# The last weight matrix in two loads instead of three, and the wait for it moved from VectorE to TensorE

## The chip, the core and the metric

The kernel runs on one core of a Trainium2 chip. The metric is the device time in microseconds of one execution; the median of 3 runs of the kernel before is 189.54 us (189.49 to 189.69). Five engines take part: TensorE (PE, with weight loads shown as PEld), VectorE (DVE), ScalarE (ACT), GpSimd (POOL) and SyncE (SP), which issues nearly all DMA transfers. The core's transfers run on 16 DMA engines.

## The reference

One token passes through an attention block with a cache of keys and values and then through a small mixer and MLP block. Cut to what matters:

```python
x = A_x                                    # 1 x 1 x 512
h = x + attention(layernorm(x))            # 32 heads, 8 key heads, 16384 cached positions of 128
g0, g1, g2, g3 = shifted pieces of gelu(layernorm(h) @ w1)   # shifted along a sequence of length 1
x1 = h + concat(g0, g1, g2, g3) @ w2
h2 = gelu(layernorm(x1) @ w3) @ w4         # w3: 512 x 1792, w4: 1792 x 512
out = h + (x1 + h2)
```

With a sequence of one token every shift leaves zeros, so that the product with w2 is zero and x1 = h; the kernel loads neither w1 nor w2. What is left of the second block is the layer norm of h, the product with w3, the gelu, the product with w4 and the sums.

## The kernel before

The kernel streams 64 MB of keys and values, four pairs of key heads one after the other, and keeps the attention's weights and the last two matrices in the buffers that the keys used. For each pair, VectorE transposes the keys (L656), TensorE makes scores (L667), a softmax follows, and TensorE multiplies with the values (L708). The loop over the pairs on TensorE is a rolled loop with a register for the count that it waits for; the rest is straight code.

The order of the work is the order of the program: a small class records every operation with what it reads and writes, and puts before each instruction the waits for the semaphores of what it needs (on the same engine only where that is not in order anyway). Each load has a semaphore of its own, and one load counts as landed when all of its parts have landed. All loads of the tail go through the queue of SP, in the order in which they are written: `wo` in two loads, `w3` in one, `w4` in three. They are issued once the last keys have been read from the buffer that they overwrite, long before they are used.

The tail, behind the last values: VectorE gathers the attention's output, TensorE multiplies it with `wo` (L794), h is summed (L806), the norm's sums and square roots are made on VectorE (L540 to L582) while TensorE multiplies with `w3` (L819). Some matmuls whose result nobody reads (L518, `unread`) lie between. ScalarE then makes the gelu in two halves of 7 row blocks (L829), VectorE transposes each half into `hcol` (L833), and TensorE multiplies with `w4` (L845). `w4` has 1792 rows, held as 14 row blocks of 128 rows by 512 columns (`NHC` is 14), 128 KB each. For each block m there are four matmuls of 128 columns, one for each quarter of the output, which go to four different column groups of the array. They add onto h, which already stands in the same bank (`h_ps`). Before the last block, four weight loads stand by themselves (L841) and the block's matmuls go without theirs (`held`, L524), so that the weights are in before the wait for the block's data. Behind it, VectorE and ScalarE each copy half of the result (L852, L853) and SP stores it (L855).

What the loads' pieces are is set by these tables; `piece(W4, m)` gives the number of the load that holds block m, and key `("r", 1, len(W3) + n)` is that of load n of w4:

```python
W3 = ((0, 4),)
W4 = ((0, 8), (8, 13), (13, 14))
```

In the kernel before, the transpose of the gelu's first half also reads the key of w4's first load (the term `* (n == 0)` in L833), and the matmuls wait themselves only for the loads with a number above 0.

Of the kernel before, what the change touches and what calls it, by code (L numbers as in the profile page):

```python
# [358 lines left out]
NHC = FM // 128  # L359
# [4 lines left out]

SEEN, ROUND = 53, 28
W3 = ((0, 4),)
W4 = ((0, 8), (8, 13), (13, 14))
PAIRS = HKV // 2
WHOLE = (0, 2)
CUTS = ((0, 2, 4), (0, 4))  # L370
# [15 lines left out]
def bass_sequential_preLN__gqa_block_cached__mixer_s_mlp__decode_kernel(  # L386
# [13 lines left out]
    with ExitStack() as ctx:  # L400
# [52 lines left out]
        hg = sb("hg", [128, FQ], BF16)  # L453
        hT = sb("hT", [128, NCH, 32], FP32)
        hcol = sb("hcol", [128, NHC, 32], BF16)
# [7 lines left out]
        w4_sb = kb[1][:, NCH * FM:2 * NCH * FM].rearrange("p (m c) -> p m c", m=NHC)  # L463
# [9 lines left out]
        def load(name, dst, src, key, by="SP", also=()):  # L473
            P.op(by, lambda e: e.dma_start(dst, src), w=[key, *also], dma=name)  # L474
# [28 lines left out]
        def dve(fn, r=(), w=(), bank=(), own=None):  # L503
            return P.op("DVE", fn, r, w, bank, own=own)

        def act(fn, r=(), w=(), bank=(), own=None):
            return P.op("ACT", fn, r, w, bank, own=own)
# [4 lines left out]
        def pe(fn, r=(), w=(), bank=(), also=(), times=None, many=1):  # L512

            return P.op("PE", fn, r, w, bank, also=also, times=times, many=many)
# [6 lines left out]
        def held(e, out, lhsT, rhs, stop):  # L521
            with nc.discard():
                m = e.matmul(out, lhsT, rhs, start=False, stop=stop, skip_group_check=True).ins
            return e.add_instruction(mybir.InstMatmult(  # L524
                name=nc.get_next_instruction_name(), engine=m.engine, ins=m.ins, outs=m.outs, start_tensor_calc=False,
                stop_tensor_calc=m.stop_tensor_calc, tile_size=m.tile_size, tile_position=m.tile_position,
                bass_skip_group_check=True, ldweights=False))

        def piece(cuts, m):
            return [lo <= m < hi for lo, hi in cuts].index(True)  # L530
# [62 lines left out]
        for n in range(2):  # L593
# [8 lines left out]
            r=["ident_f", "x4"], w=["quarter"])  # L602
        pe(lambda e: e.matmul(O_ps[0][:, 0:128], quarter[:, :, :].rearrange("p q u -> p (q u)"), x4[:, :],  # L603
                              start=True, stop=True), r=["quarter"], w=[("O", 0)], bank=[("O", 0)])
# [7 lines left out]
            r=["ident_f"], w=["row32"])  # L612
        dve(lambda e: e.tensor_reduce(maskdd[:, :], ident_f[:, :].rearrange("p (n d) -> p d n", d=4), AX.X, ALU.add),
            r=["ident_f"], w=["maskdd"])
# [3 lines left out]
        for z, src, key, of, n in ((zo, row32[:, :].rearrange("p (g n h) -> p g h n", g=2, h=REP), "zo", "row32", 4),  # L618
# [6 lines left out]
            r=["hT", (("st", 0), 0), (("st", 0), 6), "wq0"] + [("v", x) for x in range(VP)], w=["xn"])  # L625
# [3 lines left out]
        for i, key in enumerate(keys):  # L629
            P.part("query", i)  # L630
            for k in range(NCH):
                pe(lambda e, k=k: e.matmul(row[:, bass.ds(P.b + P.b0, 512)], copies(xn[:, k:k + 1], 128),  # L632
                                           wq_k[:, k, bass.ds(P.c + P.c0, REP * DH)], start=(k == 0), stop=(k == NCH - 1)),
                   r=["xn"], also=[("v", x) for x in range(VP)], w=["n" if key == "mn" else key], bank=[key])
        P.part()
        for g in range(2):
            half = banks[64 * g:64 * g + 64, PAIRS * g:PAIRS * g + PAIRS, :].rearrange("p j c -> p (j c)")
            for b in range(2):
# [3 lines left out]
                    r=["n" if x == "mn" else x for x in keys[PAIRS * g:PAIRS * g + PAIRS]], w=["qcol"],  # L642
                    bank=keys[PAIRS * g:PAIRS * g + PAIRS])
        for a in range(4):
            lo, hi, at = 32 * a, 32 * a + 32, QPAD + 32 * a
# [137 lines left out]
        w4_in = B_w4.rearrange("(p m) c -> p m c", p=128)  # L783
        for n, (lo, hi) in enumerate(W4):
            load(f"w4{n}", w4_sb[:, lo:hi, :], w4_in[:, lo:hi, :], ("r", 1, len(W3) + n))
# [3 lines left out]
            r=["o_m"], w=["o_f"])  # L789
        dve(lambda e: e.tensor_copy(o_b[:, :], o_f[:, :]), r=["o_f", ("r", 0, 0)], w=["o_b"])  # L790

        for r_ in range(32):
# [3 lines left out]
                                              stop=(r_ < 4 or r_ >= 28), skip_group_check=(r_ >= 4)),  # L796
               r=["o_b"] + [("r", 0, n) for n in (piece(WO, r_),) if n], w=[("O", 0)], bank=[("O", 0)],
# [3 lines left out]
        h_ps, hkey = banks[:, 6, :], "spare0"  # L801
        for n in range(2):
            dve(lambda e, n=n: e.tensor_copy(osum[:, 256 * n:256 * n + 256], O_ps[0][:, 256 * n:256 * n + 256]),  # L803
                r=[("O", 0)], w=[("osum", n)], bank=[("O", 0)])
        for q in range(4):
            pe(lambda e, q=q: e.matmul(h_ps[32 * q:32 * q + 32, 0:128], copies(row32[:, 0:1], 32),  # L806
                                       osum[:, q * 128:(q + 1) * 128], start=True, stop=True),
               r=[("osum", q // 2), "row32"], w=[hkey], bank=[hkey])
# [4 lines left out]
            r=["hT", (S, 0)] + [("r", 1, 0)], w=["hc"])  # L813
# [3 lines left out]
        for k in range(NCH):  # L817
            for q in range(4):
                pe(lambda e, k=k, q=q: e.matmul(s_ps[32 * q:32 * q + 32, 0, 0:FQ], hc[:, k, :],  # L819
                                                w3_sb[:, k, q * FQ:(q + 1) * FQ], start=(k == 0), stop=(k == NCH - 1)),  # L820
                   r=["hc"] + [("r", 1, n) for n in (piece(W3, k),) if n], w=[("s", 0)], bank=[("s", 0)])
# [4 lines left out]
            r=["xs", (S, 6), "hr"], w=[hkey], bank=[hkey])  # L826
        for n in range(2):
            lo, hi = n * NHC // 2, (n + 1) * NHC // 2
            act(lambda e, lo=lo, hi=hi: e.activation(  # L829
                hg[:, :].rearrange("p (i m) -> p i m", m=NHC)[:, :, lo:hi],  # L830
                s_ps[:, 0, 0:FQ].rearrange("p (i m) -> p i m", m=NHC)[:, :, lo:hi],
                ACTF.Gelu_apprx_tanh, scale=s[:, 7:8]), r=[("s", 0), (S, 7)], w=[("hg", n)], bank=[("s", 0)])
            dve(lambda e, lo=lo, hi=hi: e.transpose(  # L833
                hcol[:, lo:hi, :].rearrange("p m u -> p (m u)"),
                hg[:, :].rearrange("p (i m) -> p m i", m=NHC)[:, lo:hi, :]), r=[("hg", n)] + [("r", 1, len(W3))] * (n == 0), w=[("hcol", n)])
        for m in range(NHC):
            if m == 4:
                pe(None)
            if m == NHC - 1:
                for o in range(4):  # L840
                    pe(lambda e, o=o: e.ldweights(hcol[:, NHC - 1, :], tile_position=(0, 32 * o)), r=[("hcol", 1)])  # L841
            for o in range(4):
                pe(lambda e, m=m, o=o: held(
                    e, h_ps[32 * o:32 * o + 32, 0:128], hcol[:, m, :], w4_sb[:, m, o * 128:(o + 1) * 128], True)
                    if m == NHC - 1 else e.matmul(  # L845
                    h_ps[32 * o:32 * o + 32, 0:128], hcol[:, m, :], w4_sb[:, m, o * 128:(o + 1) * 128],
                    start=False, stop=False, skip_group_check=True),
                   r=[("hcol", 2 * m // NHC)] + [("r", 1, len(W3) + n) for n in (piece(W4, m),) if n],
                   w=[hkey], bank=[hkey])


# [5 lines left out]
             r=[("fin", 0), ("fin", 1)], w=["out"], dma="out")  # L857
# [32 lines left out]
```

## Time and profile before

| what | value |
|---|---|
| median of 3 runs | 189.54 us (189.49 to 189.69) |
| profiled execution, span from first to last instruction | 188.3 us |
| median less that span | 1.24 us |
| read from HBM | 79.17 MB, 420 GB/s over the span |
| busy: PE, DVE, ACT, POOL | 66%, 62%, 7%, 2% |
| mean granted TensorE clock | 0.916 of full speed |
| tail: w4's matmuls, first start to last end | 185.34 to 186.78 us |

All times of the profile are counted from the start of its span. A row of the timeline holds the start, the time from the first start to the last end of the merged instructions, the engine, the line, the operation, output and inputs with their shapes, and the count; in brackets stands the idle time of the engine before it and what ended it. In a row of stretches the columns are the stretch, its length, then busy time and count for PE, PEld, DVE, ACT and POOL, the granted clock, the share of the DMA engines and their GB/s. In the chain of waits, a DMA's piece runs from its issue to its landing. A row of DMA issues gives the size and the time from issue to landing.

### The profile page before, as it was taken

Reading aid. Unit: us, or ns where it says so; the run is one execution under the profiler, and the core shown is the slowest. Engines: PE = TensorE matmul, PEld = TensorE weight load, DVE = VectorE, ACT = ScalarE, POOL = GpSimd, SP = SyncE. Lnnn points to the kernel's source line nnn. Section 1 sums busy time; section 2 is a strip of 40 time slices with the busy share of each in tenths; the row PEclk is TensorE's granted clock in tenths of the full one; section 3 lists DMA queues with packets and bytes.
Section 4 is the critical chain, followed back from the end, with each engine's and each line's share of the span. In section 5 each row is a group of like instructions: output and inputs, shape, how many; then the busy total and the mean of one; then the engine's idle time right before and its main releaser. Section 6 shows DMA issues by size and latency. Waiting matters only on the chain.

```text
span 188.3 us, 2375 instructions
## 1 busy us (share of the span) xinstructions
PE 124.1 (66%) x760; PEld 48.3 (26%) x761; DVE 115.8 (62%) x138; ACT 13.7 (7%) x21; POOL 4.6 (2%) x8
## 2 busy tenths in 40 slices
PE   0109700698979978897910019799799889775772
PEld 0104200233322522332500003333244333222221
DVE  5730741999636998936300069993699898633173
ACT  3000200000004000004000000000400000500012
POOL 8100000000000000000000000000000000000000
PEclk9999985569999999999995557999999999999999
DMA  7999999999799999987999999998999996999994
GB/s 252 445 418 445 445 445 446 445 445 445 334 445 446 445 557 418 418 390 334 446 445 445 445 446 445 445 445 334 445 446 445 543 390 292 445 432 411 433 429 193
DMA packets 2607, 79.19 MB, mean 421 GB/s; under 512 B 302, under 2 KB 430, under 8 KB 686
## 3 DMA queue, kind: packets, MB, share of 16 engines
q1 hardware_dynamic: 2598, 79.17, 98.0%
q8 instruction: 1, 0.02, 0.0%
q10 hardware_dynamic: 8, 0.00, 0.0%
HBM read 79.17 MB, written 0.00 MB: 420 GB/s over the span
## 4 chain that ended last, share of the span: by engine, by line
DMA 69%; DVE 23%; PE 4%; issue 3%; SPq 1%; DVEq 0%
DMA kb<-in_A_k_cache_dram 54%; DVE kt L656 22%; DMA kb<-in_B_w_dram 15%; PE banks L667 3%; SPq L474 1%; PE banks L845 0%; DVE fin L852 0%; DVEq L147 0%; DVE den L725 0%; PE banks L524 0%; DVE od L723 0%; SPq L147 0%
## 5 line engine op out<-in xcount | busy, mean ns | idle before, releaser
L667 PE MATMUL banks<-kt,qn 128*128 x256 | 68.1, 401 | 36.8 <-DVE kt L656 35.7
L656 DVE STREAM_TRANSPOSE kt<-kb 128x2048 int32<-128x2048 int32 (+2 forms) x24 | 70.6, 2994 | 27.5 <-DMA kb<-in_A_k_cache_dram 26.4
L667 PEld LDWEIGHTS banks<-kt,qn 128*128 x256 | 25.4, 100 | 79.4 <-issue 65.5
L518 PE MATMUL banks<-qb 128*128 128x512 bf16 x61 | 22.1, 387 | 0.7 <-issue 0.2
L708 PE MATMUL banks<-vb,pt 128*32 128x512 bf16 x256 | 14.7, 379 | 1.1 <-POOLq L500 1.1
L693 ACT ACTIVATE p_sb<-banks,bias 128x1024 bf16<-128x1024 f32 x4 | 4.5, 1114 | 133.3 <-DVE nmh L688 133.3
L632 PE MATMUL banks<-vb,xn 128*128 x32 | 8.5, 432 | 6.7 <-DVE xn L623 6.7
L697 DVE STREAM_TRANSPOSE pt<-p_sb 64x1024 bf16<-64x1024 bf16 x8 | 9.9, 1239 | 4.4 <-ACT p_sb L693 4.3
L681 DVE TENSOR_REDUCE mx<-banks 128x1 f32<-128x1024 f32 x4 | 4.9, 1224 | 10.5 <-PE banks L667 10.5
L518 PEld LDWEIGHTS banks<-qb 128*128 128x128 bf16 x62 | 5.9, 97 | 16.0 <-issue 15.7
L708 PEld LDWEIGHTS banks<-vb,pt 128*32 128x32 bf16 x256 | 8.5, 97 | 5.4 <-POOLq L500 1.2
L639 DVE STREAM_TRANSPOSE qcol<-banks 64x1024 f32<-64x1024 f32 x4 | 4.8, 1227 | 6.7 <-PE banks L632 6.7
L632 PEld LDWEIGHTS banks<-vb,xn 128*128 128x128 bf16 x32 | 3.5, 108 | 11.4 <-issue 8.7
L676 ACT ACTIVATE banks<-mean 128x1024 f32<-128x1024 f32 x4 | 4.1, 1027 | 18.6 <-DVE qcol L639 18.5
L684 PE MATMUL banks<-mxd,mean 128*128 128x128 f32 x8 | 2.0, 326 | 4.7 <-DVE mxd L682 4.7
L732 DVE SCALAR_TENSOR_TENSOR od<-banks,rowc,od 128x128 f32<-128x128 f32 x12 | 4.2, 350 | 0.4
L794 PE MATMUL banks<-kb,o_b 128*32 128x512 bf16 x44 | 3.3, 384 | 1.6 <-DVE o_b L790 1.1
L729 DVE TENSOR_SCALAR od<-banks,rowc 128x128 f32<-128x128 f32 x4 | 1.3, 319 | 4.6 <-PE banks L708 4.6
L603 PE MATMUL banks<-x,quarter 4*128 4x128 bf16 x1 | 0.3, 286 | 5.4 <-DVE quarter L601 5.4
L601 DVE CAST quarter<-ident_f 4x128 bf16<-4x128 f32 x1 | 2.9, 2901 | 1.3 <-DMA x<-in_A_x_dram 1.3
L737 PE MATMUL banks<-od,zo 128*32 128x128 f32 x10 | 2.0, 283 | 1.8 <-DVE od L732 1.6
L803 DVE COPY osum<-banks 128x256 f32<-128x256 f32 x2 | 0.8, 418 | 4.0 <-PE banks L794 4.0
(74 smaller groups left out, 39.5 us busy)
## 6 DMA issues: line engine op xcount, KB each, us to landing
kb<-in_A_k_cache_dram SPq DMA_DIRECT2D x4, 4096.0 KB, 20.5
vb<-in_A_wq_dram SPq DMA_DIRECT2D x1, 3584.0 KB, 11.7
kb<-in_A_wo_dram SPq DMA_DIRECT2D x1, 2560.0 KB, 26.2
kb<-in_B_w_dram SPq DMA_DIRECT2D x1, 1792.0 KB, 24.4
kb<-in_A_wo_dram SPq DMA_DIRECT2D x1, 1536.0 KB, 29.5
kb<-in_B_w_dram SPq DMA_DIRECT2D x1, 1024.0 KB, 26.6
kb<-in_B_w_dram SPq DMA_DIRECT2D x1, 640.0 KB, 27.7
vb<-in_A_wq_dram SPq DMA_DIRECT2D x1, 512.0 KB, 3.6
```

Source lines behind the costliest of these rows:

```text
L518: P.op("PE", lambda e: e.matmul(O_ps[1][:, :], field[:, 0:128], field[:, 0:512], start=True, stop=True), r=["qb"], bank=[("O", 1)], times= ...
L632: pe(lambda e, k=k: e.matmul(row[:, bass.ds(P.b + P.b0, 512)], copies(xn[:, k:k + 1], 128), wq_k[:, k, bass.ds(P.c + P.c0, REP * DH)], sta ...
L639: dve(lambda e, g=g, b=b, half=half: e.transpose(qcol[64 * g:64 * g + 64, 2 * b:2 * b + 2, :, :].rearrange("p e m u -> p (e m u)"), half.r ...
L656: P.op("DVE", lambda e, t=t, n=n: e.transpose(pieces(kt, t, n).bitcast(I32), pieces(kb[y], t, n).bitcast(I32)), r=[("r", y, i) for i in ra ...
L667: pe(lambda e, n=n: e.matmul(row[:, bass.ds(P.y, 512)], qn[:, n, bass.ds(P.q, 128)], key_piece(P.k, n), start=False, stop=(n == 3), skip_g ...
L676: act(lambda e: e.activation(s_all, copies(mean4[:, 0:1], 1024), ACTF.Identity, scale=0.0), r=["mean4", "p"], w=[("s", 0), ("s", 1)], **both)
L681: dve(lambda e: e.tensor_reduce(mx[:, :], s_all, AX.X, ALU.max), r=[("s", 0), ("s", 1)], w=["mx"], **both)
L693: act(lambda e: e.activation(p_sb[:, :], s_all, ACTF.Exp, bias=bias[:, 0:1], scale=float(SCALE), accum_out=acc[:, :]), r=[("s", 0), ("s", ...
L697: dve(lambda e, g=g: e.transpose(pt[64 * g:64 * g + 64, :, :, g, :], p_sb[64 * g:64 * g + 64, :]), r=["p"], w=["pt"])
L708: pe(lambda e, l=l, ct=ct, ch=ch: e.matmul(O_ps[0][32 * ct:32 * ct + 32, :], pt[:, l, ch, :, :].rearrange("p g u -> p (g u)"), tiles[:, l ...
L732: dve(lambda e, block=block, c=c: e.scalar_tensor_tensor(od[:, :], block, rowc[:, c:c + 1], od[:, :], ALU.mult, ALU.add), r=[key, "rowc", ...
L794: pe(lambda e, r_=r_, q=q: e.matmul(O_ps[0][32 * q:32 * q + 32, :], copies(o_b[:, r_:r_ + 1], 32), wo_sb[:, r_ * D:(r_ + 1) * D], start=(r ...
```

## The change

w4 comes in two loads, of blocks 0 to 11 and of blocks 12 and 13. The transposes of the gelu no longer read the key of w4's first load; every matmul of the last product reads the key of the load that holds its block. The weight loads that stand by themselves, and the matmuls without theirs, move from block 13 to block 12, the first of the last load; block 13 behind it is made of common matmuls, and the accumulation's end mark moves to it.

```diff
-W4 = ((0, 8), (8, 13), (13, 14))
+W4 = ((0, 12), (12, 14))
...
             dve(lambda e, lo=lo, hi=hi: e.transpose(
                 hcol[:, lo:hi, :].rearrange("p m u -> p (m u)"),
-                hg[:, :].rearrange("p (i m) -> p m i", m=NHC)[:, lo:hi, :]), r=[("hg", n)] + [("r", 1, len(W3))] * (n == 0), w=[("hcol", n)])
+                hg[:, :].rearrange("p (i m) -> p m i", m=NHC)[:, lo:hi, :]), r=[("hg", n)], w=[("hcol", n)])
         for m in range(NHC):
             if m == 4:
                 pe(None)
-            if m == NHC - 1:
+            if m == W4[-1][0]:
                 for o in range(4):
-                    pe(lambda e, o=o: e.ldweights(hcol[:, NHC - 1, :], tile_position=(0, 32 * o)), r=[("hcol", 1)])
+                    pe(lambda e, m=m, o=o: e.ldweights(hcol[:, m, :], tile_position=(0, 32 * o)), r=[("hcol", 1)])
             for o in range(4):
                 pe(lambda e, m=m, o=o: held(
-                    e, h_ps[32 * o:32 * o + 32, 0:128], hcol[:, m, :], w4_sb[:, m, o * 128:(o + 1) * 128], True)
-                    if m == NHC - 1 else e.matmul(
+                    e, h_ps[32 * o:32 * o + 32, 0:128], hcol[:, m, :], w4_sb[:, m, o * 128:(o + 1) * 128], False)
+                    if m == W4[-1][0] else e.matmul(
                     h_ps[32 * o:32 * o + 32, 0:128], hcol[:, m, :], w4_sb[:, m, o * 128:(o + 1) * 128],
-                    start=False, stop=False, skip_group_check=True),
-                   r=[("hcol", 2 * m // NHC)] + [("r", 1, len(W3) + n) for n in (piece(W4, m),) if n],
+                    start=False, stop=(m == NHC - 1), skip_group_check=True),
+                   r=[("hcol", 2 * m // NHC), ("r", 1, len(W3) + piece(W4, m))],
```

On SP, the last rows of the queue, from wo's second load on (`d_w40`, `d_w41`, `d_w42` below are the semaphores of w4's loads, `d_k1` that of the keys in the same buffer; a load of 128x4096 is 4096 elements of 2 bytes in each of 128 rows):

```order
 L474 DMA kb<-in_A_wo_dram 128x6144
 L474 DMA kb<-in_B_w_dram 128x7168 [waits e_DVE,d_k1]
-L474 DMA kb<-in_B_w_dram 128x4096
-L474 DMA kb<-in_B_w_dram 128x2560
-L474 DMA kb<-in_B_w_dram 128x512
+L474 DMA kb<-in_B_w_dram 128x6144
+L474 DMA kb<-in_B_w_dram 128x1024
 L855 DMA out_dram<-fin 2x2x128 [waits e_both]
```

Three loads of 1024, 640 and 128 KB became two of 1536 and 256 KB at the same place behind w3, and the first of them is as large, and has rows as long, as wo's second.

On TensorE, where the product with w4 begins (`e_DVE` is the semaphore that VectorE's instructions count up, `e_ACT` that of ScalarE's):

```order
 L819 MATMUL banks<-kb,hc 32x448 x15
-L845 MATMUL banks<-kb,hcol 32x128 [waits e_DVE]
+L845 MATMUL banks<-kb,hcol 32x128 [waits d_w40,e_DVE]
 L845 MATMUL banks<-kb,hcol 32x128 x15
 L344 COMPARE_AND_BRANCH
```

The wait for the first load now stands before the first of the 56 matmuls, beside the wait for the transposes.

On TensorE, from block 4 to the end of the product:

```order
 L845 MATMUL banks<-kb,hcol 32x128 x12
 L845 MATMUL banks<-kb,hcol 32x128 [waits e_DVE]
-L845 MATMUL banks<-kb,hcol 32x128 x3
-L845 MATMUL banks<-kb,hcol 32x128 [waits d_w41]
 L845 MATMUL banks<-kb,hcol 32x128 x19
 L841 LDWEIGHTS hcol x4
-L524 MATMUL banks<-kb,hcol 32x128 [waits d_w42]
+L524 MATMUL banks<-kb,hcol 32x128 [waits d_w41]
 L524 MATMUL banks<-kb,hcol 32x128 x3
+L845 MATMUL banks<-kb,hcol 32x128 x4
```

The wait before block 8 is gone, and the wait for the last load stands before block 12 with one more block behind it.

## The prediction

> **What bounds the kernel now.** I read the chain of waits first, then its last piece, then the timeline of that piece. The page's summary of the chain says how the whole run is bound:
>
> ```profile
> DMA 69%; DVE 23%; PE 4%; issue 3%; SPq 1%; DVEq 0%
> ```
>
> Nearly all of it is the stream of keys, values and weights from HBM, which the change leaves alone. The change touches what stands at the end of the chain. The chain in order of time, from 157.68 us on:
>
> ```profile
> 157.68 0.33 SPq L474
> 158.01 0.05 issue
> 158.06 0.43 SPq L474
> 158.48 0.05 issue
> 158.53 27.68 DMA kb<-in_B_w_dram
> 186.22 0.04 issue
> 186.26 0.46 PE banks L845 x20
> 186.73 0.07 PE banks L524 x4
> ```
>
> The load issued at 158.53 is the second of the three of w4 (blocks 8 to 12). It lands 27.68 us later, at 186.22, TensorE starts 0.04 us after, and the output follows. So the end hangs on landings and on the matmuls that are left behind the last landings. The page's list of DMA issues gives the landings of all four last loads:
>
> ```profile
> kb<-in_B_w_dram SPq DMA_DIRECT2D x1, 1792.0 KB, 24.4
> kb<-in_B_w_dram SPq DMA_DIRECT2D x1, 1024.0 KB, 26.6
> kb<-in_B_w_dram SPq DMA_DIRECT2D x1, 640.0 KB, 27.7
> kb<-in_B_w_dram SPq DMA_DIRECT2D x1, 128.0 KB, 27.5
> ```
>
> With the issue times of the chain: w3 (1792 KB) lands at 157.68 + 24.4 = 182.1, blocks 0 to 7 at 158.06 + 26.6 = 184.66, blocks 8 to 12 at 186.22. The last is issued behind those: 158.53 + 0.43 + 0.05 = 159.0, if its predecessor's issue takes as long as the one before it; + 27.5 gives 186.5. The timeline of the tail shows who waited for each:
>
> ```profile
> 183.65 0.85 ACT L829 ACTIVATE hg<-banks,st 128x224 bf16<-128x224 f32 x2 [0.75 <-PE banks L819]
> 184.71 1.05 DVE L833 STREAM_TRANSPOSE hcol<-hg 128x224 bf16<-128x224 bf16 x2 [1.04 <-DMA kb<-in_B_w_dram]
> 185.34 0.71 PE L845 MATMUL banks<-kb,hcol 128*32 128x128 bf16 x32 [1.75 <-DVE hcol L833]
> 186.26 0.46 PE L845 MATMUL banks<-kb,hcol 128*32 128x128 bf16 x20 [0.20 <-DMA kb<-in_B_w_dram]
> 186.56 0.22 PE L524 MATMUL banks<-kb,hcol 128*32 128x128 bf16 x4
> 186.82 0.27 ACT L853 ACTIVATE fin<-banks 64x128 bf16<-64x128 f32 x1 [2.32 <-PE banks L524]
> ```
>
> VectorE's transposes wait for the first load (to 184.71), TensorE's first 32 matmuls for the transposes (to 185.34); they are through at 185.34 + 0.71 = 186.05, and TensorE then idles 0.20 us for the second load. That idle gap is the first thing to see: **the transposes' wait is real, but it is not on the path that sets the end**. Its slack is 0.20 us. The other thing is at 186.56: 0.04 us after the last landing, the last four matmuls start; without that wait they would have started one step (0.055 us, below) behind the fifth block, at about the same time. Both landings end together for the end.
>
> **The change part by part.**
>
> *Transposes without the load's wait.* The gelu's two ACT instructions run 183.65 to 184.50. The first of two transposes then starts some 0.1 us after the first ACT half, near 184.2, instead of 184.71, and both are done about 1.05 us later, at 185.3. TensorE's start came 0.63 us behind the first transpose's (184.71 to 185.34), so hcol's first half is ready for it at 184.8 and the second by 185.3. The gain on the end is nothing, since TensorE's new first wait, for the load, ends later than both (next). Were that cover gone, the transposes would cost those 0.63 us. Nothing else is queued behind them on VectorE but the final CAST.
>
> *When 12 blocks have landed.* This is the term that decides, and I bound it in two ways. From the two landings here: 640 KB separate 184.66 from 186.22, that is 1.56 us for five blocks or 0.312 us a block. Four blocks behind the first landing is 184.66 + 1.25 = 185.91; one block ahead of the second is 186.22 − 0.31, the same 185.91. From a load of the same size and row length that this kernel already makes, the second of wo (the timeline's rows, then the page's):
>
> ```profile
> 147.92 0.80 SPq L474 DMA_DIRECT2D kb<-in_A_wo_dram  x2
> 157.68 1.77 SPq L474 DMA_DIRECT2D kb<-in_B_w_dram  x4
> 177.88 0.83 PE L794 MATMUL banks<-kb,o_b 128*32 128x512 bf16 x12 [0.53 <-DMA kb<-in_A_wo_dram]
> ```
>
> ```profile
> kb<-in_A_wo_dram SPq DMA_DIRECT2D x1, 2560.0 KB, 26.2
> kb<-in_A_wo_dram SPq DMA_DIRECT2D x1, 1536.0 KB, 29.5
> ```
>
> wo's first load lands at 147.92 + 26.2 = 174.1 and the reader of its second starts at 177.88, so that landed at 177.84: 3.7 us for 1536 KB behind its predecessor. Behind w3's 182.1 the twelve blocks then land at 185.8. Between 185.8 and 185.91 I take the middle, 185.85: the higher one comes from loads with shorter rows than the new load's, the lower one from landings that are rounded to 0.1 us. The lag of a landing behind its bytes is in both. It can be seen at the end:
>
> ```profile
> 184.60:184.80 0.20, 0.00 (x0) 0.00 (x0) 0.09 (x1) 0.00 (x0) 0.00 (x0) 1.00 0.98 410
> 185.80:186.00 0.20, 0.20 (x14) 0.10 (x4) 0.00 (x0) 0.00 (x0) 0.00 (x0) 1.00 0.64 220
> 186.00:186.20 0.20, 0.06 (x4) 0.00 (x0) 0.00 (x0) 0.00 (x0) 0.00 (x0) 1.00 0.04 10
> 186.20:186.40 0.20, 0.14 (x12) 0.14 (x16) 0.00 (x0) 0.00 (x0) 0.00 (x0) 1.00 0.00 0
> ```
>
> The last columns are the DMA share and GB/s: bytes stop near 186.05, while the last landing is seen at 186.5, 0.45 us later. [...]
>
> *What TensorE does from there.* All 14 blocks, 56 matmuls, now stand behind that landing, where 24 stood behind the second load before. Each block is four matmuls side by side; the timeline cut at three places gives its step:
>
> ```profile
> 186.26 0.24 PE L845 MATMUL banks<-kb,hcol 128*32 128x128 bf16 x4 [0.20 <-DMA kb<-in_B_w_dram]
> 186.26 0.46 PE L845 MATMUL banks<-kb,hcol 128*32 128x128 bf16 x20 [0.20 <-DMA kb<-in_B_w_dram]
> 185.34 0.57 PE L845 MATMUL banks<-kb,hcol 128*32 128x128 bf16 x28 [1.75 <-DVE hcol L833]
> ```
>
> One block takes 0.24, five 0.46, seven 0.57: 0.055 us a further block. Fourteen take 0.24 + 13 × 0.055 = 0.96 us, the jump after block 3 included, as it lay within the seven. Start: 185.85 + 0.04 = 185.89. End: 186.85. Before, the last four ended at 186.56 + 0.22 = 186.78. So **+0.07 us**.
>
> *The new waits.* At its start TensorE now waits for the transposes and the load, one behind the other; the first is over by then. The waits at block 7 (second transpose) and block 12 (second load) find their condition met: 185.3 against 185.89 + 0.4, and the second load is the end of the same 1792 KB as before, so it lands at 186.5 or a little earlier, against block 12 at 185.89 + 0.02 + 12 × 0.055 = 186.57. A met wait isn't in the trace; its bounds are nothing and the 0.04 us from a landing to a start. I take 0.01 for all. Should the second load land as late as 186.5, cover is 0.03 us, and without it the end moves by as much as the landing does.
>
> *One load and 128 rows fewer.* SP issues three loads instead of four in a row (row of 1.77 us); the queue is over 24 us deep there, so nothing waits for it. It can bring the last landing forward by what the 128 short rows lose: 128 KB at the 410 GB/s of the stretch ahead are 0.32 us, which is what separates the last two landings already (186.22 to 186.5), so under 0.1 us. None of it counts, since the end now hangs on the first load. It bounds a gain, though: block 13 can't start before the last landing, at earliest 186.4, + 0.04 + 0.055, and 0.22 for it makes 186.71, −0.07 us on 186.78.
>
> Sum: 0.07 + 0.01 = +0.08 us. The profiled span is 188.3, to which 1.24 us around it are added to give the 189.54 of the runs; the sum is a difference within the span and goes on 189.54: **189.62 us**. With 185.8 for the landing and nothing for the waits it is +0.02, with 185.91 and both waits at 0.04 it is +0.21.
>
> **The rivals.**
>
> *The clock falls in the longer gap (slower).* TensorE now idles from 183.6 to 185.89 instead of 185.34 (the first row, of the timeline, is its last work ahead; the others are stretches).
>
> ```profile
> 182.66 0.94 PE L819 MATMUL banks<-kb,hc 128*32 128x448 bf16 x16 [0.33 <-ACT hc L812]
> ```
>
> ```profile
> 183.96:187.37 3.41, 1.23 (x56) 0.85 (x56) 1.34 (x3) 0.82 (x3) 0.00 (x0) 1.00 0.58 229
> 187.37:188.30 0.93, 0.00 (x0) 0.00 (x0) 0.00 (x0) 0.00 (x0) 0.00 (x0) 0.50 0.01 1
> 182.46:185.87 3.41, 1.47 (x48) 0.79 (x48) 2.05 (x7) 1.29 (x4) 0.00 (x0) 1.00 0.98 403
> ```
>
> The clock (third column from the right) fell to 0.50 at 187.37, after 3.41 us in which TensorE was busy for 1.23. In 182.46 to 185.87 it was busy 1.47, of which 0.53 from 185.34 on goes away: 0.94, less than 1.23. If a fall comes at such a moment, the 14 blocks run at half clock. The price is bounded by rows of the key loop:
>
> ```profile
> 37.18:40.60 3.42, 3.42 (x9) 1.17 (x8) 0.50 0.71 307
> 50.84:54.25 3.41, 3.40 (x15) 1.23 (x13) 1.00 0.89 384
> ```
>
> Nine matmuls against 15 is a factor of 1.7; on 13 × 0.055 = 0.72 us that is +0.5, at a factor of two +0.72. The time would be 190.1 to 190.35. Against it: the fall must come within the 1 us before the end, of 3.41 us, and no row shows a fall inside a stretch that was busy on both sides. [...]
>
> *The twelve blocks land with the last (slower).* If the two loads share the 16 engines rather than follow each other, the first is complete only with the end, up to 186.5. TensorE would end at 186.5 + 0.04 + 0.96 = 187.50, +0.72 us, 190.26; halfway, +0.36, 189.90. It decides once the first landing is past 186.15. Against it: landings stand in the order and at the spacing of their bytes.
>
> *The shorter chain shows (faster).* If executions without the profiler have their loads earlier against the gelu, the transposes are the path, and up to 0.63 us goes: 188.9. Against it: the transposes have 0.20 us of slack, and the load would have to come 0.6 us earlier to fall behind them. Or the load fewer takes off its 0.1 us: 189.45, no measurable change.
>
> **How the numbers follow.** A measurement of this kernel tells 0.2%, 0.38 us, from no change. The forecast, +0.08 with bounds of +0.02 and +0.21, lies well within: chance 0.76, own range 189.45 to 189.8 with the scatter of the runs shown (189.49 to 189.69). The clock has 0.08 and the shared loads 0.08, half of the latter under 0.38 us; the shorter chain 0.08, most of it under 0.38 us too. Faster 0.06, within 0.82, slower 0.12. The range reaches up into both slow rivals: 189.38 to 189.95.
>
> **What would show it.** In the profile after, the transposes start near 184.2 with ACT as releaser; TensorE's one gap ends on the DMA at 185.8 to 185.95; one row of L845 matmuls without idle gaps follows, 0.9 to 1.0 us to the last of them, with no idle before block 12; the output's ACT and CAST start at 186.85 to 186.95. It is wrong if that gap ends past 186.1, if TensorE waits again for the second load, if the clock reads 0.50 ahead of the end, or if the transposes still end TensorE's wait.

## The result, and the profile after

The changed kernel takes 189.75 us (median of 22 runs, 189.53 to 190.51), the kernel before 189.47 us (189.28 to 189.91) beside it: a ratio of 1.0016, 95% interval 1.0010 to 1.0023. That is 0.30 us slower (0.0016 × 189.47; interval 0.19 to 0.44), less than the 0.38 us that the prediction took as the bound of no change, but clear of zero and well over the 0.08 us forecast. Measured again beside the experiments, it came to 1.0020 (1.0005 to 1.0035).

The end of the chain of waits after:

```profile
157.56 0.33 SPq L474
157.89 0.05 issue
157.94 27.66 DMA kb<-in_B_w_dram
185.60 0.14 issue
185.74 1.28 PE banks L845 x48
187.01 0.11 PE banks L524 x4
187.12 0.12 PE banks L845 x4
```

The chain now goes through the load of twelve blocks, as forecast, and it lands 27.66 us after its issue, at 185.60. w3 lands 0.23 us earlier here than in the profile before (its landings in the two traces are 181.89 and 182.12), so 185.60 stands for 185.83 there: 185.85 was forecast. What follows was not: 0.14 us to the first matmul instead of 0.04, and 1.28 + 0.11 + 0.12 = 1.51 us of matmuls instead of 0.96. The timeline of the tail:

```profile
184.48 1.04 DVE L833 STREAM_TRANSPOSE hcol<-hg 128x224 bf16<-128x224 bf16 x2
185.74 1.28 PE L845 MATMUL banks<-kb,hcol 128*32 128x128 bf16 x48 [1.92 <-DMA kb<-in_B_w_dram]
186.76 0.36 PE L524 MATMUL banks<-kb,hcol 128*32 128x128 bf16 x4
186.87 0.36 PE L845 MATMUL banks<-kb,hcol 128*32 128x128 bf16 x4
187.27 0.28 DVE L852 CAST fin<-banks 64x128 bf16<-64x128 f32 x1 [1.74 <-PE banks L845]
```

The transposes run without a wait for a load, and TensorE's one gap of 1.92 us ends on the DMA. There is no second wait for the last load. But a block's four matmuls, 0.24 us before, take 0.36. The clock shows why (third column from the right):

```profile
182.58:185.99 3.41, 1.50 (x37) 0.69 (x41) 2.49 (x11) 0.97 (x3) 0.00 (x0) 1.00 0.85 351
185.99:187.24 1.25, 1.24 (x52) 0.97 (x40) 0.00 (x0) 0.00 (x0) 0.00 (x0) 0.50 0.05 13
```

In this execution the granted clock fell to 0.50 at 185.99, 0.25 us into the product, after 3.41 us in which TensorE was busy for 1.50. That is the prediction's first rival. It does not happen in every execution: a second profile of the same kernel, below, has the clock at 1.00 to the end of the product. So the question was how much of the 0.30 us is the clock and what the rest is.

### The profile page after: what moved, and what is told of

Read it like the earlier page. It is cut to its first block, busy times and chain, and to the rows that moved or that the text cites. A ratio compares the mean times of both kernels' runs of the same rounds, so it can differ in the third digit from the quotient of the medians.

```text
span 188.7 us, 2375 instructions
## 1 busy us (share of the span) xinstructions
PE 127.3 (67%) x761; PEld 49.5 (26%) x761; DVE 116.2 (62%) x138; ACT 13.7 (7%) x21; POOL 4.6 (2%) x8
## 4 chain that ended last, share of the span: by engine, by line
DMA 68%; DVE 26%; issue 3%; PE 1%; SPq 1%; DVEq 0%
DMA kb<-in_A_k_cache_dram 54%; DVE kt L656 26%; DMA kb<-in_B_w_dram 15%; PE banks L845 1%; SPq L474 1%; DVE fin L852 0%; DVEq L147 0%; PE banks L524 0%; DVE den L725 0%; DVE od L723 0%
## 5 line engine op out<-in xcount | busy, mean ns | idle before, releaser
L632 PE MATMUL banks<-vb,xn 128*128 x32 | 9.6, 473 | 6.6 <-DVE xn L623 6.6
L794 PE MATMUL banks<-kb,o_b 128*32 128x512 bf16 x44 | 4.7, 559 | 1.1 <-DVE o_b L790 1.1
```

The source lines that it names most:

```text
L794: pe(lambda e, r_=r_, q=q: e.matmul(O_ps[0][32 * q:32 * q + 32, :], copies(o_b[:, r_:r_ + 1], 32), wo_sb[:, r_ * D:(r_ + 1) * D], start=(r ...
```

## The experiments

All edits leave the output as it is. The theory after the result had three terms: a longer row of matmuls behind the landing (+0.05 to +0.07), a dearer wait in front of it (+0.09), and falls of the clock in some executions. Spans are given beside times, since the span ends with the last instruction and some edits act behind it.

**The two parts apart.** First the wait alone, with the three loads kept:

```diff
+W4 = ((0, 8), (8, 13), (13, 14))          # the rest as in the changed kernel
```

> The kernel before with the second part of the change alone: the transposes wait for no load and TensorE waits itself, but w4 comes in the three loads of 8, 5 and 1 blocks. All theories: the last block still starts 0.04 us behind the last landing and the fifth block behind the second, so the end does not move: 189.47, at most 0.05 away. The first product starts near 184.85 instead of 185.34. If the clock falls in the tail of the kernel before too, the shorter gap makes it rarer and the median falls by up to 0.1.

Measured: ratio 1.0006 (0.9996 to 1.0017), no difference that shows. Its timeline has the idle gap ahead of the second load grown to 0.72 us:

```profile
184.53 0.71 PE L845 MATMUL banks<-kb,hcol 128*32 128x128 bf16 x32 [1.21 <-DVE hcol L833]
185.96 0.46 PE L845 MATMUL banks<-kb,hcol 128*32 128x128 bf16 x20 [0.72 <-DMA kb<-in_B_w_dram]
186.26 0.22 PE L524 MATMUL banks<-kb,hcol 128*32 128x128 bf16 x4
```

The first matmuls start earlier, and the time so gained is waited away at the second load. So the transposes' old wait cost nothing, as the prediction read it. Then the loads alone, with the transposes still waiting for the first:

```diff
-W4 = ((0, 8), (8, 13), (13, 14))
+W4 = ((0, 12), (12, 14))                  # r=[..., ("r", 1, len(W3))] of the first transpose kept
```

> The kernel before with the first part of the change alone: two loads of 12 and 2 blocks, and the transposes wait for the first. The cover of the transposes is gone: landing 185.85, + 0.05 to the transposes, + 0.63 to the first matmul, + 0.96 for 56 matmuls = 187.49 against 186.78, +0.7 us, 190.2. As the gap on TensorE is then 2.9 us, the clock theory expects the clock to fall in more of the executions, with up to 0.7 us more in those: 190.2 to 190.6. The queue rival, that the end hangs on the last landing alone, expects +0.1.

Measured: ratio 1.0071 (1.0058 to 1.0084), +1.35 us (1.10 to 1.59): at or above the upper end of the +0.7 to +1.1 that the clock theory gave.

```profile
185.66 1.05 DVE L833 STREAM_TRANSPOSE hcol<-hg 128x224 bf16<-128x224 bf16 x2 [2.23 <-DMA kb<-in_B_w_dram]
186.29 0.93 PE L845 MATMUL banks<-kb,hcol 128*32 128x128 bf16 x48 [2.95 <-DVE hcol L833]
187.39 0.28 DVE L852 CAST fin<-banks 64x128 bf16<-64x128 f32 x1 [0.68 <-PE banks L845]
```

In this profile the clock held through the product (0.93 us for 48 matmuls), and the output starts 5.52 us after w3's landing (187.39 − 181.87) against 4.70 before: +0.82, the 0.7 of the sum and a little more. It was the shortest of the five, with a span of 188.9; the others are 189.3 to 189.8, up to 0.9 us longer. That fits a clock that falls in the gap of 2.95 us, but their clock inside the product was not seen, so the cause of what goes beyond +0.82 is argued, not shown. The second part of the change is thus what makes the first bearable: it hides the transposes' 0.6 us (0.63 from the first transpose's start to the first matmul here, 185.66 to 186.29).

**The wait in front of the product.** The trace after shows on TensorE an instruction that the trace before has not, a semaphore instruction of 0.05 us at 185.63, between the landing at 185.60 and the first weight load at 185.71. The first matmul has two waits there. This edit gives its weight loads the wait for VectorE and leaves it the load's:

```diff
-            if m == W4[-1][0]:
+            if m in (0, W4[-1][0]):
                 for o in range(4):
-                    pe(... e.ldweights(hcol[:, m, :], ...), r=[("hcol", 1)])
+                    pe(... e.ldweights(hcol[:, m, :], ...), r=[("hcol", 2 * m // NHC)])
```

> The changed kernel with the weights of block 0 loaded by four instructions of their own that wait for VectorE, so that the first matmul waits for the load alone. Double-wait theory: in the profile after, TensorE's first weight load comes 0.11 us behind the landing (185.60 to 185.71), against 0.04 us where one wait stood before, because one of two waits became an instruction of its own (0.05 us at 185.63). With one wait the gap is 0.04 us again and the median falls by 0.06 to 0.07 us to 189.68. Rival: the 0.11 us is the wake-up of an engine that was idle for 1.9 us, and it stays.

Measured: ratio 1.0010 (0.9997 to 1.0022). The interval alone doesn't tell it from the changed kernel, but its chain and timeline do:

```profile
157.89 27.63 DMA kb<-in_B_w_dram
185.52 0.04 issue
185.56 0.22 PE banks L524 x4
```

```profile
185.56 0.22 PE L524 MATMUL banks<-kb,hcol 128*32 128x128 bf16 x4 [2.27 <-DMA kb<-in_B_w_dram]
186.29 0.22 PE L845 MATMUL banks<-kb,hcol 128*32 128x128 bf16 x4
186.57 0.28 DVE L852 CAST fin<-banks 64x128 bf16<-64x128 f32 x1 [1.66 <-PE banks L845]
```

From landing to matmul it is 0.04 us again, though TensorE had been idle for 2.27 us, longer than in the changed kernel. So it is the second wait that costs, not a wake-up. Nor is it that the weights were already in: the second load of the kernel before has the same 0.04 us (186.22 to 186.26), and its weights are loaded behind the landing. The changed kernel measured again gives the same end with two waits and no fall of the clock:

> The changed kernel itself, on the chip of this call, as the base for the two with fillers: 0.2 to 0.35 us slower than the kernel before, with some times above 190.

```profile
158.20 27.65 DMA kb<-in_B_w_dram
185.85 0.14 issue
185.99 0.85 PE banks L845 x48
186.84 0.06 PE banks L524 x4
186.90 0.08 PE banks L845 x4
186.97 0.02 issue
187.00 0.28 DVE fin L852
```

Counted from w3's landing, which no edit touches, to the start of the output:

| kernel, clock at 1.00 in the product | w3 landed | output starts | between | against before |
|---|---|---|---|---|
| before | 182.12 | 186.82 | 4.70 us | |
| changed, one wait ahead of the product | 181.82 | 186.57 | 4.75 us | +0.05 |
| changed | 182.15 | 187.00 | 4.85 us | +0.15 |
| changed, clock fallen in the product | 181.89 | 187.27 | 5.38 us | +0.68 |

The longer row of matmuls costs 0.05 us, the second wait 0.10, a fall of the clock at that moment 0.53. The profiles of the runs below in which the clock stood at 1.00 in the product and nothing else delayed it repeat the first two: 4.84 to 4.86 us in three with two waits, 4.73 in one with one wait, 4.70 in two with the three loads of before (4.68 in the run with the wait alone).

**The clock, first try.** Six unread matmuls were put into TensorE's gap:

```diff
+        for n in range(6):
+            unread(None)
         for m in range(NHC):
```

> The changed kernel with six matmuls of 512 columns, whose result nobody reads, between the product with w3 and that with w4, so that TensorE is busy until about 185.1 instead of 183.8. Clock theory: part of the +0.28 us (189.75 against 189.47) comes from executions in which the clock falls inside the last product, as in the profiled one (0.50 from 185.99 on). The fillers keep each 3.4 us stretch busier than that one's 1.50 us, so the high times (190.2 to 190.5) go, the granted clock reads 1.00 until the product is over, and the median falls to 189.60 to 189.68. Rival, the queue: the loss lies in the landing and in the longer row of matmuls alone; fillers change nothing, 189.75.

Measured: ratio 1.0172 (1.0156 to 1.0187), 3.2 us slower, a clear miss that neither theory had. The timeline shows one place:

```profile
185.74 0.85 PE L847 MATMUL banks<-kb,hcol 128*32 128x128 bf16 x48 [0.54 <-DMA kb<-in_B_w_dram]
186.41 0.24 PE L524 MATMUL banks<-kb,hcol 128*32 128x128 bf16 x4
186.46 0.24 PE L847 MATMUL banks<-kb,hcol 128*32 128x128 bf16 x3
189.62 0.26 PE L847 MATMUL banks<-kb,hcol 128*32 128x128 bf16 x1 [2.92 <-issue]
```

The very last matmul starts 2.92 us after the others, waiting for nothing that the profile shows. The clock was at 1.00 until 189.34. The page's list of queues has a transfer of instructions:

```profile
q8 instruction: 1, 0.02, 0.0%
```

In this trace that transfer of 16 KB starts at 186.96, behind the next-to-last matmul, takes 1.33 us and is over 1.33 us before the last matmul starts. The traces before and after have one such transfer near their end too (it starts at 187.20 and 186.91), so it does not show by itself that the matmul waited for it. A second entry, q14, is on the page of this run alone, and the expectation that follows takes it for the cause; but it is a transfer of 72 bytes at 0.10 us, at the start of the program, and says nothing about the end. The reading, which rests on the runs that follow and not on a queue: the twelve instructions that make TensorE's code longer delay its last one. That it fell outside what was loaded is my guess; no view shows it. The following four runs had fewer fillers, or as many elsewhere:

> The changed kernel with four unread matmuls in the gap, where six made the last matmul start 2.92 us late (186.70 to 189.62, with a load of instructions on a queue of its own). Code-position theory: six fillers are 12 instructions and one instruction fell outside what was loaded, so four (8 instructions) leave the end whole: no gap in the last row of matmuls. Clock theory: TensorE is then busy for about 1.9 us of any 3.4 us around the gap instead of 1.50, the clock holds until the product is over, and the median is 0.1 us or more under the changed kernel's of the same call, with fewer times above 190. Rival: the clock plays no part in the median, and the two are within 0.05.

> The kernel before with the same four fillers. Clock theory: its gap is shorter and only the last 24 matmuls stand behind the last landings, so a fall costs it less and comes less often; the fillers gain under 0.05 us: 189.35. Rival: the fillers help by taking part in something else (order of fetches, bank), and it gains or loses as much as the changed kernel.

> The changed kernel with both repairs: block 0's weights loaded ahead, so that one wait stands before the first matmul, and four fillers for the clock. The two terms add up: what is left against the kernel before is the longer row of matmuls alone, +0.03 to +0.07 us (56 matmuls in 0.96 us behind the landing of twelve blocks): ratio 1.0002 to 1.0004. If more than +0.12 is left, something else makes the change slower.

> The changed kernel with four unread matmuls put ahead of the product with wo, 11 us before the end, where TensorE is idle for 1 us. They are as many instructions as in the gap before the last product, and none of them is near it. Code theory: the time outside the span grows by 1 us, as with the four in the gap (2.1 to 2.4 us), and the clock falls as in the changed kernel (spans of 188.2 to 189.3): median 190.6 to 190.8. Rival: fillers in the gap delayed the program's end by their own work, and these cost nothing: 189.75.

| kernel | ratio to before | median span | median of the time outside the span |
|---|---|---|---|
| before, beside all of these | 1 | 188.1 to 188.2 | 1.30 to 1.34 |
| changed, 4 fillers in the gap | 1.0063 (1.0047 to 1.0079) | 188.35 | 2.2 |
| changed with one wait, 4 fillers in the gap | 1.0056 (1.0037 to 1.0075) | 188.15 | 2.2 |
| before, 4 fillers in the gap | 1.0018 (1.0007 to 1.0029) | 188.15 | 1.7 |
| changed, 4 fillers 11 us earlier | 1.0059 (1.0038 to 1.0080) | 188.6 | 1.9 |

With four, no matmul is late, but the time outside the span grows by 0.3 to 0.9 us, wherever in the tail's code the fillers stand: the last row's are far from the end, and it grows by 0.6 all the same, while its spans stay near those of the changed kernel. With six, the time outside the span was 1.29 us, as before: there the delay lies inside the span. So the length of TensorE's code moves these times, and not a filler's own work in the gap. The first three runs miss their forecasts for that reason; the fourth comes close to its own (190.59 us for 190.6 to 190.8). Why the kernel before loses 0.3 us and the changed one 0.9, and what is waited for outside the span, the profiles don't show. For the span alone the fillers can still speak of the clock:

| | executions | spans of 188.7 us or more |
|---|---|---|
| before, beside all experiments | 75 | 6 |
| changed, both measurements | 34 | 11 |
| changed, with or without the second wait, 4 fillers in the gap | 12 | 1 |
| before, 4 fillers in the gap | 12 | 0 |
| changed, 4 fillers 11 us earlier | 6 | 3 |
| changed with one wait, no fillers | 12 | 2 |
| the wait alone (three loads), no fillers | 12 | 1 |
| loads alone (gap of 2.95 us, no cover) | 5 | 5 |

The long spans are four times as frequent in the changed kernel (32% against 8%). With fillers in the gap they are fewer, but 12 executions are too few to show that the fillers did it: with one wait and no fillers there are 2 in 12. The mean granted clock, on record for every execution, is a better witness. It is 0.892 to 0.895 in 7 of the changed kernel's 11 long executions (0.893 in the profiled one), in 3 of its 23 others, and under 0.896 in none of the 75 of the kernel before. The other four long ones have 0.901 to 0.910, like the six long ones of the kernel before, and their cause stays open. The stream also moves the span: in the profile of the changed kernel with four fillers in the gap, w3 landed at 182.32, 0.20 us later than in that of before, and the span was 188.6 with the clock at 1.00 in the product. In 23 executions below 188.7 the changed kernel's median span is 188.3, that of before 188.1 (69 executions).

**The clock, with code of even length.** The two unread matmuls behind the product with wo were taken out, and three put into the gap, two of them without a weight load:

```diff
-        for n in range(2):
-            unread(None)
         h_ps, hkey = banks[:, 6, :], "spare0"
...
+        unread(None)
+        for n in range(2):
+            pe(lambda e: held(e, O_ps[1][:, :], qb[:, 0, 0, 0:128], ...[:, 0:512], True), r=["qb"], bank=[("O", 1)])
         for m in range(NHC):
```

> The changed kernel with the two unread matmuls behind the product with wo taken out and three put behind the product with w3, two of them without a weight load of their own, so that TensorE's code is no longer than before. Four fillers had brought every span to 188.2 to 188.6 (changed kernel: 188.2 to 189.3), but the time outside the span had grown by 1 us. Code theory: that growth came from the longer code; with even code the time outside the span is 1.25 to 1.4 us again. Clock theory: with 0.8 us of filler the falls inside the last product become rare, spans at 188.7 or more go from 11 in 34 to 1 in 12 or fewer, and the median is 189.55 to 189.62, 0.1 to 0.15 under the changed kernel's 189.72 to 189.75. Rival to the clock: the same share of spans at 188.7 or more, and 189.7.

> The same even code with block 0's weights loaded ahead, so that one wait stands before the first matmul: another 0.07 to 0.09 us less, 189.45 to 189.55, that is 0.0 to 0.1 over the kernel before. If both repairs hold, this leaves the longer row of matmuls, +0.03 to +0.07.

> The kernel before with the same even code. Clock theory: its last 24 matmuls lose little to a fall, so at most 0.05 us are gained, 189.37 to 189.45, with fewer times above 189.8. If it gains 0.1 or more, the kernel before pays for the clock too.

Measured: changed 1.0011 (1.0000 to 1.0022), changed with one wait 1.0001 (0.9991 to 1.0011), before 1.0001 (0.9989 to 1.0013). The time outside the span is 1.31 to 1.33 again in all three: the code theory holds. The changed kernel has 2 in 12 long spans, one more than forecast, its median of 189.66 us is above the 189.55 to 189.62 forecast, and its ratio can't be told from 1.0016; the gain has the sign of the clock theory and no more. With both repairs the change is even with the kernel before, which agrees with the +0.05 us that is left. None of these beats the kernel before. The edit is not a clean test of the clock, since it takes work away 5 us earlier: in the profile with one wait the clock was at 0.50 from 182.97 to 186.38, and the product with w3 took 1.68 us (0.94 in the changed kernel with the same even code), the two fillers without a weight load 1.06 (0.59 there):

```profile
183.39 1.68 PE L817 MATMUL banks<-kb,hc 128*32 128x448 bf16 x16 [1.28 <-ACT xs L820]
185.41 1.06 PE L524 MATMUL banks<-qb 128*128 128x512 bf16 x2
186.40 0.23 PE L524 MATMUL banks<-kb,hcol 128*32 128x128 bf16 x4
```

Here the product waited for the slow fillers and then ran at the speed of the profile with one wait alone (0.78 us for its 44 matmuls in both).

## Why the prediction was right or wrong

The 189.75 us measured lie within the range of the prediction, but in part by luck: of the 0.30 us, the sum's main term explains 0.05. Another 0.10 is a wait that the sum put at 0.01, and the rest, by the estimate below, a rival that was given a chance of 0.08.

*What bounds the end: right.* The slack of 0.20 us ahead of the second load was real. Taking the transposes' wait away alone moved nothing (1.0006). The cover in the changed kernel was thinner than forecast: its transposes ran from 184.48 to 185.52, not from 184.2 to 185.3, and ended 0.08 us ahead of the landing.

*The landing of twelve blocks: right.* 185.83 on the scale of the profile before, against 185.85. The load of the same size and row length (wo's second, 3.7 us behind its predecessor) was the better of the two bounds: the new load came 3.71 us behind w3. The rival of shared loads fell with it: the second lands 0.6 us after the first, at 186.24.

*The row of 14 blocks: right.* 0.85 + 0.06 + 0.08 us in the chain of the execution with a steady clock; the term came out at +0.05 for +0.07.

*The new waits: wrong, and the step that failed.* "I take 0.01 for all" with an upper bound of 0.04 each. The two waits that stand together cost 0.10 us: one of them becomes an instruction of its own that runs only after the landing (0.05 us at 185.63, the landing at 185.60). I counted only waits that were already met as harmless, which holds at blocks 7 and 12, and overlooked that the pair at block 0 is worked off one after the other behind the later of the two.

*The clock: a rival with 0.08 that happened in part.* Its picture, a fall behind 3.41 us with little work ahead of the product, came true in the profiled execution, though not its number: 0.94 us was reckoned, and the profile after has 1.49 (182.33 to 185.74), since the unread matmuls and the product with w3 ran later there (the product starts 0.99 us behind w3's landing, not 0.54). The share of moments at which the fall can strike, estimated at 1 us of 3.41 or about 30%, is near the 32% of long spans, though the kernel before has 8% too. Its price was set at 0.5 to 0.72; measured 0.53. By the prediction's own sign, a clock of 0.50 ahead of the end, the profiled execution went the rival's way. What was missed is that this was no case of all or none: a share of executions has it. As an estimate from the two tables, the excess share of 24% (32 − 8) at 0.53 us is 0.13 us on the mean, and with the 0.15 us of the steady clock that makes 0.28, against 0.30 measured. That the long spans are falls inside the product is inferred: one such execution was profiled, and six more have a mean clock like it. In the profiled execution a stretch of 3.41 us ended inside the product, at 185.99 (earlier in that trace the clock was at 0.50 for just such a stretch, 175.76 to 179.17). In the changed kernel's second profile they end elsewhere, at 185.29 and 188.70 (the first row is a stretch long before the tail):

```profile
164.81:168.22 3.41, 2.34 (x12) 0.67 (x15) 1.59 (x3) 0.43 (x2) 0.00 (x0) 1.00 1.12 482
181.87:185.29 3.42, 2.25 (x22) 0.76 (x22) 2.70 (x14) 1.54 (x4) 0.00 (x0) 1.00 0.95 401
185.29:188.70 3.41, 0.96 (x56) 0.82 (x56) 0.82 (x3) 0.27 (x1) 0.00 (x0) 1.00 0.16 59
```

The stretch ahead of the product was busy 2.25 us, the clock held, and it fell at 188.70, when all was done. In the first profile a stretch of 1.50 ended at 185.99 and the clock fell. The busy time alone is not what decides, though: in the second profile the clock fell to 0.50 at 168.22 too, behind the first row's 2.34 us, and in the kernel before it held behind 1.80 us (170.30 to 173.72). What the clock counts stays open.

*The shorter chain (faster): fell,* by the run with the wait alone.

## What to carry to other kernels

One load fewer gained nothing here: the row of matmuls that then stands behind the larger load cost 0.05 us. Taking away a wait gains nothing while another ends later (1.0006). Put one wait, not two, in front of the first instruction behind a landing (0.10 us here): give the earlier one to a weight load or to another instruction ahead of it. The gap of 1.9 us on TensorE near the end of this kernel was a bet on the clock, which fell at 185.99 in one of its two profiles and held through the product in the other: read a spread of times, not one profile. Judge an added instruction only against code of equal length (eight more cost 0.3 to 0.9 us outside the span here), and look at the time outside the span as well as at the span.

## What the runs showed of the hardware that was not expected

- Two waits on one TensorE instruction cost 0.10 us more from landing to start than one (0.14 us in the chains of four traces, 0.04 in that with one wait), although the other condition had been met before (by the transposes, 0.08 us ahead of the landing in the profile after).
- The clock fell after a 3.41 us stretch in which TensorE was busy for 1.50 us, and held after one of 1.80 us (170.30 to 173.72 in the kernel before). Busy time alone doesn't sort the stretches: in the changed kernel's second profile the clock also fell after 2.34.
- Twelve more TensorE instructions came with 2.9 us in front of the last matmul, and eight with 0.3 to 0.9 us more outside the span; with code of equal length the time outside the span was 1.31 to 1.33 us again. What is waited for was not seen.
